# A fused local-and-pooled attention with a tanh-shrink MLP: dense blocks that follow the batches, V tiles every 112 tokens, V pooled on TensorE, nine-token rows of q and k, and weights cast by DMA

## The chip, the core and the metric

The kernel runs on one core of a Trainium2 chip. Its engines work side by side, each on its own list of instructions in order: TensorE (PE in the profile; matmuls, with weight loads shown apart as PEld), VectorE (DVE), ScalarE (ACT), GpSimd (POOL) and SyncE (SP), which here issues DMAs. The metric is the time of one execution in microseconds; lower is better.

## What is computed

```python
def _attn_ref(q, k, v):                       # 8 batches, 8 heads, 576 tokens, 64 wide
    q_d, k_d, v_d = means over groups of 4 tokens (144 groups)
    out_d = softmax_attention(q_d, k_d, v_d)  # pooled attention
    out_up = np.repeat(out_d, 4, axis=2)
    mask = np.abs(pos[:, None] - pos[None, :]) < 4
    out_local = softmax_attention(q, k, v, masked by mask)
    return out_up + out_local

def _moe_ref(x, w_in, w_out):                 # x: 4608 tokens x 512
    h = x @ w_in                              # to 2048
    g = h - np.tanh(h)
    return g @ w_out                          # back to 512
```

Inputs and the output are float32; the kernel computes its products in bfloat16 with float32 sums.

## The kernel before

**Work.** Attention goes in 32 pairs of heads, four pairs to a batch (pair p belongs to batch p // 4). The dense part, the two products of the MLP, goes in nine blocks of 512 tokens. All instructions are entered as operations with the tiles they read and write, a cost and a priority (class Program); a planner lays them out by simulated start times, and each engine gets its list in that order. Attention has the priority 10 x p, dense matmuls 5000 (so they fill what attention leaves), the dense blocks' ACT and DVE steps -1.

**A pair of attention.** SP loads q and k (load_qk, L291) as 96 rows of six tokens and V (load_v, L310 to L316) as five overlapping windows of 128 tokens, 120 apart. prep_v (L351) casts V to bf16 on POOL or ACT. The casts at L416 bring q and k to bf16. Then there are two forms:

- Old form, pairs 0 to 15: TensorE transposes q and k in twelve pieces (L442), ACT copies them out of PSUM (L448). V is pooled on TensorE for two pairs at a time (pool_v, L389 and L391, six matmuls with 128 output rows against `pick`), and ACT copies the result (L396). Local scores for tiles 0 to 3 (s1, L478), then the last tile and the pooled scores (s2, L478 and L494), are computed one after the other into the same banks `ps_ts`. The normalised output is transposed back on TensorE (back, L566 to L570), ACT copies the pooled part (L597), and DVE joins the two into `xT` (L599).
- New form, pairs 16 to 31 (T_DMA, X_DMA, NEW): q and k are transposed by a DMA that SP issues (L424), ACT copies them into token order (L432). V is loaded a second time in rows of four tokens (load_v4, L362) and pooled by two additions on POOL (pool_v4, L372 and L376). Both kinds of scores are computed in one go (s12), the second kind into `ps_ox`. The output is transposed by a DMA (L573) and joined on DVE or POOL (L582, L588).

In both, q and k are pooled by two additions (L459, L464), ACT takes the exponentials (L511, L521, L524), DVE masks them (L514, L527), TensorE forms the outputs (L538, L545), and DVE divides (L554, L556).

**Dense blocks.** mm1 (L619) multiplies `w_in` by `xT`: 16 groups of four matmuls of 512 columns a block, each into one of four PSUM banks `ps_hy`; ACT takes tanh (L627), DVE subtracts (L630) into `gT`, of which there are two. mm2 (L646) multiplies `gT` by `w_out`: 4 groups of 16 matmuls; ACT copies (L657) and SP stores (L660). Block k needs every batch that its 512 tokens touch. Block 0 is entered as 16 groups of mm1 and then its mm2; block 1 as mm1 alone; from block 2 on, mm1 of a block alternates with mm2 of the block before. The banks are handed out in turn in this order, so a step also waits for the earlier user of its bank.

**Weights.** SP loads `w_in` after the first four pairs (L328) and `w_out` between later pairs (L335, L337), in float32, into space borrowed from `gT` and `xT`. POOL and ACT cast them (load_w, L344), 32 pieces of 128 x 512.

Ahead of the first dense matmul, TensorE also runs filler matmuls (L802) where the plan leaves it idle.

Of the kernel before, what the change touches and what calls it, by code (L numbers as in the profile page):

```python
# [150 lines left out]
def kernel(  # L151
# [18 lines left out]
    A6 = 6  # L170
    G6 = S // A6
    QW = 120
    NT = 5
    NQ = [120, 120, 120, 120, 96]
    KOFF = 585
    N_FF = Dff // 128
    N_DC = Dm // 128
    NBLK = NTOK // 512
# [13 lines left out]
    pick = fixed("pick", [128, 6, 128], BF16)  # L192
# [4 lines left out]
    qkn = fixed("qkn", [G6, 2, 2, A6 * D], FP32, NQKN)  # L197
# [3 lines left out]
    qr = fixed("qr", [G6, 2, A6, 128], BF16, 2)  # L201
    qk = fixed("qk", [128, 1192], BF16, 2)
    qT = fixed("qT", [128, 2, A6, G6], BF16, 2)
    half = fixed("half", [128, 2, G, 2], FP32)
    qkd = fixed("qkd", [128, 344], BF16, 2)
    v4 = fixed("v4", [72, 2, 2, 4 * D], FP32, 2)
    v2 = fixed("v2", [72, 2, 2, 2 * D], FP32)
    vp = fixed("vp", [72, 2, 2, D + 1], BF16, 2)
    E = fixed("E", [128, 1840], BF16, 2)
# [5 lines left out]
    gT = fixed("gT", [128, N_FF, 512], BF16, 2)  # L215
# [37 lines left out]
    def c_pick():  # L253

        V.memset(pick, 0.0)
        for t in range(4):
            V.tensor_copy(out=pick[:, t, 30 * t:30 * t + 30], in_=group[:, 1:31])
        V.tensor_copy(out=pick[:, 4, 120:128], in_=group[:, 1:9])
        V.tensor_copy(out=pick[:, 5, 112:128], in_=group[:, 9:25])

    def c_mask():

        GP.memset(mask, 1.0)
        m4 = mask[:, 0:480].rearrange("p (t c) -> p t c", c=QW)
        for part, pat in ((m4, [[0, 4], [1, QW]]),
                          (mask[:, 480:576], [[1, 96]])):
            neg = [[-s, n] for s, n in pat]
            GP.affine_select(
                out=part, in_=part, compare_op=ALU.is_ge, fill=0.0,
                base=-1, pattern=neg, channel_multiplier=1)  # L270
            GP.affine_select(
                out=part, in_=part, compare_op=ALU.is_ge, fill=0.0,
                base=7, pattern=pat, channel_multiplier=-1)
        GP.affine_select(
            out=mask[:, 0:QW], in_=mask[:, 0:QW], compare_op=ALU.is_ge,
            fill=0.0, base=-4, pattern=[[0, QW]], channel_multiplier=1)
        GP.affine_select(
            out=mask[:, 480:576], in_=mask[:, 480:576], compare_op=ALU.is_ge,
            fill=0.0, base=99, pattern=[[0, 96]], channel_multiplier=-1)
# [6 lines left out]
    def load_qk(p):  # L286

        b, h0, s = p // NP, 2 * (p % NP), p % NQKN
        for i, src in enumerate((q, k)):
            def issue(i=i, src=src):  # L290
                nc.sync.dma_start(  # L291
                    out=qkn[s][:, i], in_=src[b, h0:h0 + 2].rearrange(
                        "h (g a) d -> g h (a d)", a=A6))
            load(500, issue, [("qkn", s, i)], T_QK, -30)

    def load_v(p):

        b, j, s = p // NP, p % NP, p % NVST
        t = vst[s]
        for i in range(2):  # L300
            h = 2 * j + i
            base = v[b, h]

            def win(tok, n, nt, base=base):
                return bass.AP(tensor=base.tensor, offset=base.offset + tok * D,
                               ap=[[D, n], [QW * D, nt], [1, D]])

            def issue(h=h, i=i, win=win):
                if b == 0 and h == 0:
                    nc.sync.dma_start(out=t[4:128, i, 0, :], in_=v[b, h, 0:124, :])  # L310
                    nc.sync.dma_start(out=t[:, i, 1:5, :], in_=win(QW - 4, 128, 4))
                elif b == B - 1 and h == H - 1:
                    nc.sync.dma_start(out=t[0:100, i, 4, :], in_=v[b, h, 476:576, :])
                    nc.sync.dma_start(out=t[:, i, 0:4, :], in_=win(-4, 128, 4))
                else:
                    nc.sync.dma_start(out=t[:, i], in_=win(-4, 128, 5))  # L316
            if (b, h) in ((0, 0), (B - 1, H - 1)):
                def clear(h=h, i=i):
                    part = t[0:32, i, 0, :] if h == 0 else t[96:128, i, 4, :]
                    V.memset(part, 0.0)  # L320
                op("DVE", 100, clear, writes=[("vst", s, i)], pri=-99)
            load(1000, issue, [("vst", s, i)], T_V, -30)

    def load_w(src, dst, name, f, stage, keys):

        def issue():
            if src is moe_w_in:
                nc.sync.dma_start(out=stage.rearrange("p (c f) -> p c f", c=4),  # L328
                                  in_=src[:, 512 * f:512 * f + 512].rearrange(
                                      "(c p) f -> p c f", p=128))  # L330
            else:
                rows = src.rearrange("(f p) n -> p f n", p=128)
                if isinstance(stage, list):
                    for c in range(4):
                        nc.sync.dma_start(out=stage[c], in_=rows[:, 4 * f + c, :])  # L335
                else:
# [497 lines left out]
```

## Time and profile before

| | |
|---|---|
| median of 3 runs | 348.71 us (348.31 to 348.74) |
| span of the profiled execution, first to last instruction | 346.3 us |
| mean granted TensorE clock | 0.984 |
| matmuls | 2556, of them 1152 dense |
| moved by DMA | 60.74 MB, nearly all issued by SP |

Times in the profile are microseconds from the first instruction. A row of instructions in order of time gives start, duration, engine, line, operation, output <- inputs, size and how many stand together; in square brackets, how long the engine had been idle and what ended that. Matmuls are pipelined: a row lasts longer than the engine needs before the next one, so what a matmul costs is read from start to start. A row of a stretch gives its length, then for each engine the busy time and the number of instructions, then the granted clock, the DMA engines' share (it can pass 1 where packets overlap) and GB/s.

### The profile page before, as it was taken

To read this page: it belongs to the slowest core of one execution; us is meant where nothing else is said; L and a number is where in the kernel's file an instruction comes from. 1 tells how busy PE (TensorE), PEld (TensorE's weight loads), DVE (VectorE), ACT (ScalarE), POOL (GpSimd) and SP (SyncE) were. 2 spreads that over 40 slices of the span, in tenths; PEclk is the share of its full clock that TensorE was granted. 3 is DMA by queue.
4 is the path that set the end of the run, shared out by engine and by line. 5 is a ranking of instruction groups with operands and counts; after the bars stand their busy time and mean duration, and the time that the engine had idled before them with its cause. 6 is when DMAs were issued, how large, how long until landed. Compare 5 with 4: busy or idle time off the path is not lost.

```text
span 346.3 us, 6847 instructions
## 1 busy us (share of the span) xinstructions
PE 328.0 (95%) x2556; PEld 163.5 (47%) x2556; DVE 223.8 (65%) x362; ACT 224.8 (65%) x382; POOL 169.9 (49%) x210
## 2 busy tenths in 40 slices
PE   6787989999999999999999999899999999999995
PEld 2353445555555554445444444444454444444442
DVE  5675788558897968778867677679774443343300
ACT  4585886768978768787878778599753434343411
POOL 6553555575467856887777786958500000000000
PEclk9698999999999999999999999999999999999999
DMA  8999999999999998999999999645231000100021
GB/s 192 234 374 300 277 262 263 217 216 287 212 222 234 252 234 174 226 231 235 261 221 207 260 233 246 157 92 93 57 85 60 31 32 30 61 32 31 30 93 61
DMA packets 103407, 60.74 MB, mean 175 GB/s; under 512 B 77774, under 2 KB 94670, under 8 KB 103374
## 3 DMA queue, kind: packets, MB, share of 16 engines
q1 hardware_dynamic: 103374, 60.30, 78.5%
q8 instruction: 20, 0.33, 0.4%
q14 instruction: 13, 0.11, 0.1%
HBM read 42.46 MB, written 9.44 MB: 150 GB/s over the span
## 4 chain that ended last, share of the span: by engine, by line
PE 69%; DVE 10%; ACT 9%; issue 3%; DMA 3%; POOL 2%; SPq 1%; ACTq 0%; POOLq 0%; DVEq 0%
PE ps_hy_540 L646 8%; PE ps_hy_538 L619 8%; PE ps_hy_539 L619 7%; PE ps_hy_541 L646 7%; PE ps_hy_538 L646 7%; PE ps_hy_539 L646 6%; PE ps_hy_540 L619 6%; PE ps_hy_541 L619 6%; PE ps_ox L538 3%; DVE qr_87 L416 2%; PE ps_ts L478 2%; DMA qkn_73<-in_k_dram 2%; PE ps_ox L545 2%; PE ps_ts L442 2%; PE ps_ox L389 2%
## 5 line engine op out<-in xcount | busy, mean ns | idle before, releaser
L619 PEld LDWEIGHTS <-w_in_sb 128*128 128x128 bf16 x576 | 53.3, 98 | 62.1 <-issue 3.9
L646 PEld LDWEIGHTS <-gT_110 128*128 128x128 bf16 x320 | 30.2, 98 | 34.5
L646 PEld LDWEIGHTS <-gT_111 128*128 128x128 bf16 x256 | 24.0, 98 | 27.4
L459 POOL TENSOR_TENSOR half<-qk_88 128x576 f32<-128x576 bf16 x14 | 16.4, 1169 | 25.3 <-ACT qk_88 L448 11.2
L459 POOL TENSOR_TENSOR half<-qk_89 128x576 f32<-128x576 bf16 x16 | 18.7, 1167 | 19.8 <-ACT qk_89 L448 12.2
L646 PE MATMUL ps_hy_539<-w_out_sb,gT_110 128*128 128x512 bf16 x80 | 20.7, 379 | 0.0
L646 PE MATMUL ps_hy_540<-w_out_sb,gT_110 128*128 128x512 bf16 x80 | 20.4, 379 | 0.0
L646 PE MATMUL ps_hy_538<-w_out_sb,gT_110 128*128 128x512 bf16 x80 | 20.4, 379 | 0.0
L646 PE MATMUL ps_hy_541<-w_out_sb,gT_110 128*128 128x512 bf16 x80 | 20.1, 379 | 0.0
L432 ACT COPY qk_89<-qT_91 128x576 bf16<-128x576 bf16 x16 | 18.7, 1193 | 0.0
L432 ACT COPY qk_88<-qT_90 128x576 bf16<-128x576 bf16 x16 | 18.4, 1188 | 0.0
L511 ACT ACTIVATE E_100<-ps_ts 128x960 bf16<-128x960 f32 x16 | 15.6, 977 | 3.8 <-PE ps_ts L478 3.8
L556 DVE TENSOR_TENSOR ln_106<-ps_ox,r_104 128x896 bf16<-128x896 f32 x16 | 17.4, 1090 | 0.5
L646 PE MATMUL ps_hy_540<-w_out_sb,gT_111 128*128 128x512 bf16 x64 | 16.9, 379 | 0.0
L646 PE MATMUL ps_hy_541<-w_out_sb,gT_111 128*128 128x512 bf16 x64 | 16.8, 379 | 0.0
L646 PE MATMUL ps_hy_539<-w_out_sb,gT_111 128*128 128x512 bf16 x64 | 16.6, 379 | 0.0
L646 PE MATMUL ps_hy_538<-w_out_sb,gT_111 128*128 128x512 bf16 x64 | 16.4, 379 | 0.0
L511 ACT ACTIVATE E_101<-ps_ts 128x960 bf16<-128x960 f32 x14 | 13.6, 973 | 3.8 <-PE ps_ts L478 3.6
L514 DVE TENSOR_TENSOR E_101<-E_101,mask 128x960 bf16<-128x960 bf16 x16 | 13.1, 820 | 3.9 <-ACT E_101 L511 3.7
L556 DVE TENSOR_TENSOR ln_107<-ps_ox,r_105 128x896 bf16<-128x896 f32 x14 | 15.3, 1090 | 0.4
L514 DVE TENSOR_TENSOR E_100<-E_100,mask 128x960 bf16<-128x960 bf16 x16 | 13.6, 847 | 2.8 <-ACT E_100 L511 2.8
L619 PE MATMUL ps_hy_538<-xT_65,w_in_sb 128*128 128x512 bf16 x36 | 13.9, 385 | 1.2 <-DVE xT_68 L599 1.2
(263 smaller groups left out, 890.1 us busy)
## 6 DMA issues: line engine op xcount, KB each, us to landing
out_dram<-y_115 SPq DMA_DIRECT2D x12, 256.0 KB, 2.6
out_dram<-y_116 SPq DMA_DIRECT2D x12, 256.0 KB, 2.3
out_dram<-y_117 SPq DMA_DIRECT2D x12, 256.0 KB, 3.0
qkn_71<-in_q_dram SPq DMA_DIRECT2D x8, 288.0 KB, 7.8
qkn_71<-in_k_dram SPq DMA_DIRECT2D x8, 288.0 KB, 5.8
qkn_72<-in_q_dram SPq DMA_DIRECT2D x8, 288.0 KB, 5.1
qkn_72<-in_k_dram SPq DMA_DIRECT2D x8, 288.0 KB, 5.5
qkn_73<-in_q_dram SPq DMA_DIRECT2D x8, 288.0 KB, 6.6
```

Of the source, the lines that this page charges most:

```text
L389: T.matmul(pv[:, 0, :], pick[:, t, :], vw[w][:, :, t, 0:64], start=(t == 0), stop=(t == NT - 1))
L416: P.choice([(eng, ns, lambda dst=dst, srt=srt, fn=fn: fn(out=dst, in_=srt)) for eng, ns, fn in REORDER[p >= NEARLY][i]], reads=[("qkn", sn ...
L432: op("ACT", 600, lambda i=i: A.copy(out=full[:, i].rearrange("p (g a) -> p g a", a=A6), in_=qT[s][:, i].rearrange("p a g -> p g a")), read ...
L442: T.transpose(b16[:, G6 * a:G6 * a + G6], qr[s][:, i, a, :], ident[0:G6, 0:G6])
L459: eng.tensor_tensor(out=half, in0=four[:, :, :, 0:2], in1=four[:, :, :, 2:4], op=ALU.add)
L478: T.matmul(sc[:, c:c + NQ[t]], qk[s][rows, k0:k0 + 128], qk[s][rows, QW * t:QW * t + NQ[t]], start=True, stop=True)
L511: op("ACT", 870, lambda: A.activation(out=e1, in_=ps[:, :, 0:480], func=AF.Exp, scale=SCALE), reads=ts, writes=[("E", s, 0)], pri=pri)
L514: op("DVE", 700, lambda: V.tensor_tensor(out=e1, in0=e1, in1=mask[:, 0:480].unsqueeze(1).to_broadcast([128, 2, 480]), op=ALU.mult), reads= ...
L538: T.matmul(po[:, hh, 65 * t:65 * t + 65], E[s][:, c:c + 128], vw[w][:, 2 * jj + hh, t, :], start=True, stop=True)
L556: op("DVE", 1010, lambda: V.tensor_tensor(out=ln[s].rearrange("p n (h d) -> p h n d", d=D), in0=blocks[:, :, :, 0:64], in1=r[s].unsqueeze( ...
L619: T.matmul(ps_hy[slot], w_in_sb[:, dc, fc * 128:(fc + 1) * 128], xT[dc][:, kb * 512:kb * 512 + 512], start=(dc == 0), stop=(dc == N_DC - 1))
L646: T.matmul(ps_hy[slot], gT[g][:, fc, ts * 128:ts * 128 + 128], w_out_sb[:, fc, :], start=(fc == 0), stop=(fc == N_FF - 1))
```

## The change

- **Dense blocks follow the batches.** Eight blocks in place of nine: even ones of 512 tokens, odd ones of 640, so that block b needs batch b and no later one. An odd block's mm1 runs in two halves of 320 columns. A block's mm1 is interleaved with mm2 of the block before by share; the last call runs mm2 of block 7 alone. A bank is taken as the one longest unused, and mm2 holds its bank until its 16 matmuls are done.
- **V tiles every 112 tokens**, all inside the head's 576, so the loads need no cleared edges and no special cases; the tiles' query ranges are 120, 112, 112, 112, 120.
- **V pooled on TensorE for all pairs**: four matmuls with 32 output rows each, into quarters of the partitions, and one with 128. Pooled q and k are laid out as 5 x 32 columns (160 in place of 144). From pair 4 on the result goes to `ps_ts`. load_v4 and pool_v4 are gone.
- **Nine-token rows**: q and k of a pair are loaded as 64 rows each of nine tokens, q on even and k on odd partitions, and transposed in nine pieces of 128 x 128. Another load form (`tok`) is in the code and no pair uses it.
- **Weights cast by DMA**: POOL issues one DMA per quarter of `w_in` and `w_out`, which casts on its way. Each waits for the V cast of a pair: `w_in` of pairs 2, 2, 3, 3 and `w_out` of pairs 3, 4, 5, 6.
- **The new form from pair 10** in place of 16 (DMA transposes on both sides, scores in one go).
- The planner's costs are new numbers.

The core of the diff:

```diff
-    M2_FIRST, T_DMA, X_DMA, NEW = 16, 16, 16, 16
+    EARLY = 10
+    TIN = ['pe'] * EARLY + ['dma'] * (NPAIR - EARLY)
+    MERGE = [False] * EARLY + [True] * (NPAIR - EARLY)
+    XOUT = ['pe'] * EARLY + ['dma'] * (NPAIR - EARLY)
+    W_IN_AT, W_OUT_AT = (2, 2, 3, 3), (3, 4, 5, 6)
...
+    def span(kb):
+        return (kb * S, 512, 1) if kb % 2 == 0 else (kb * S - 64, 320, 2)
+
+    def take():
+        slot = next(x for x in slots if x not in held)
+        slots.remove(slot)
+        slots.append(slot)
+        return slot
...
     def dense(kb):
+        n1 = 16 * span(kb)[2] if kb < B else 0
+        n2 = 16 + 4 * ((kb - 1) % 2) if kb else 0
+        steps = sorted([((i + 0.5) / n1, 0, i) for i in range(n1)] +
+                       [((i + 0.5) / n2, 1, i) for i in range(n2)])
+        for _, second, i in steps:
+            if second:
+                mm2(kb - 1, i)
+            else:
+                mm1(kb, i)
...
     def load_w(src, dst, name, f, gate):
+        op("POOL", 1000, lambda: nc.gpsimd.dma_start(out=to, in_=rows),
+           reads=[gate], writes=[("wq", name, f)], pri=-40)
+        op("DMA", T_W, None, reads=[("wq", name, f)],
+           writes=[(name, f, c) for c in range(4)], pri=-30)
...
     def pool_v(hb):
-            for t in range(NT):
-                T.matmul(pv[:, 0, :], pick[:, t, :], vw[w][:, :, t, 0:64],
-                         start=(t == 0), stop=(t == NT - 1))
-            T.matmul(pv[:, 1, :], pick[:, 5, :], vw[w][:, :, 4, 0:64],
+            for t in range(4):
+                T.matmul(pv[32 * t:32 * t + 32, 0, :], pick[:, 0:32],
+                         vw[w][:, :, t, 0:64], start=True, stop=True)
+            T.matmul(pv[:, 1, :], pick[:, 32:160], vw[w][:, :, 4, 0:64],
                      start=True, stop=True)
...
+                def put(i=i, planes=planes):
+                    if LOAD[p] == 'row':
+                        A.copy(out=full[:, i].rearrange("p (g a) -> p g a", a=A9),
+                               in_=planes[:, :, i::2].rearrange("p a g -> p g a"))
...
     def s2(bank=ps):
             for hh in range(2):
-                score(4, hh, 512 * hh, sc)
+                score(4, hh, bank[:, hh, 0:120])
             for i in range(2):
                 for hh in range(2):
                     rows = slice(64 * hh, 64 * hh + 64)
+                    T.matmul(bank[:, hh, 120 + GW * i:120 + GW * i + GW],
+                             qkd[s][rows, 1, 32 * i:32 * i + 128],
+                             qkd[s][rows, 0], start=True, stop=True)
```

More of the change, by code (lines that the diff above doesn't have):

```diff
@@ L639, in mm2 @@
         if part == 0:
[L640 to L641 removed]
+            ycur[0] = take()
+            held.append(ycur[0])
         slot = ycur[0]
```

496 lines of the change are left out of this document (214 added, 282 removed).

## The prediction

> **What bounds it now.** I read the page's totals, its slices and its chain first, then the busy time of each engine in stretches cut where the data say so, then TensorE's instructions in order of time.
>
> ```profile
> span 346.3 us, 6847 instructions
> ...
> PE 328.0 (95%) x2556; PEld 163.5 (47%) x2556; DVE 223.8 (65%) x362; ACT 224.8 (65%) x382; POOL 169.9 (49%) x210
> ...
> DMA  8999999999999998999999999645231000100021
> ...
> PE 69%; DVE 10%; ACT 9%; issue 3%; DMA 3%; POOL 2%; SPq 1%; ACTq 0%; POOLq 0%; DVEq 0%
> ...
> L432 ACT COPY qk_89<-qT_91 128x576 bf16<-128x576 bf16 x16 | 18.7, 1193 | 0.0
> ```
>
> TensorE is busy for 95% of the span and carries 69% of the chain that ended last; no other engine passes 65%. The DMA queues are near full for the first two thirds. The next views split the time. The borders are the first dense matmul (32.06), the end of the last join of batch 1 (74.90), of batch 3 (130.90) and of batch 7 (260.90), and the last matmul's end (342.10); the last column but two is the granted clock.
>
> ```profile
> core 0: us, PE busy (x) PEld busy (x) DVE busy (x) ACT busy (x) POOL busy (x), PEclk, DMA share, GB/s
> ...
> 32.06:74.90 42.84, 41.81 (x374) 21.85 (x374) 29.62 (x44) 30.88 (x59) 24.67 (x32) 0.96 1.16 253
> 74.90:130.90 56.00, 55.14 (x559) 30.53 (x558) 46.55 (x75) 43.81 (x83) 35.98 (x41) 1.00 1.14 239
> 130.90:260.90 130.00, 127.23 (x1007) 62.06 (x1005) 100.31 (x150) 99.55 (x154) 91.08 (x102) 1.00 0.89 183
> 260.90:342.10 81.20, 81.20 (x377) 36.62 (x375) 26.72 (x40) 30.40 (x53) 0.00 (x0) 1.00 0.12 45
> ```
>
> The same stretches for the first dense product (L619) alone, then for the second (L646):
>
> ```profile
> 32.06:74.90 42.84, 16.80 (x64) 6.12 (x63) 0.96 1.16 253
> 74.90:130.90 56.00, 28.27 (x112) 9.43 (x112) 1.00 1.14 239
> 130.90:260.90 130.00, 63.38 (x247) 22.60 (x246) 1.00 0.89 183
> ```
>
> ```profile
> 32.06:74.90 42.84, 15.19 (x62) 5.42 (x63) 0.96 1.16 253
> 74.90:130.90 56.00, 12.11 (x47) 4.04 (x46) 1.00 1.14 239
> 130.90:260.90 130.00, 63.04 (x248) 23.18 (x247) 1.00 0.89 183
> ```
>
> The last stretch holds nothing but dense work: 377 matmuls in 81.20 us, so 0.2154 us for one of 512 columns and no idle time at all. The program has 1,152 of them: 248.1 us. From 32.06 to 342.10 are 310.0 us, so 61.9 us went to everything else, attention's own matmuls and stalls. By stretch: 42.84 - 126 x 0.2154 = 15.7; 56.00 - 159 x 0.2154 = 21.8; 130.00 - 495 x 0.2154 = 23.4; the missing 1.0 is matmuls that cross a border and are counted twice. What attention needs on TensorE is read from starts in a stretch without gaps:
>
> ```profile
> 84.97 0.39 PE L478 MATMUL ps_ts<-qk_88 64*128 64x120 bf16 x8
> 85.29 0.33 PE L538 MATMUL ps_ox<-vw_81,E_101 128*128 128x65 bf16 x5
> ...
> 85.86 0.38 PE L619 MATMUL ps_hy_539<-xT_65,w_in_sb 128*128 128x512 bf16 x1
> ...
> 87.15 0.68 PE L442 MATMUL ps_ts<-ident,qr_87 96*128 96x96 bf16 x12
> 87.67 0.38 PE L619 MATMUL ps_hy_539<-xT_67,w_in_sb 128*128 128x512 bf16 x1
> ...
> 88.10 0.22 PE L566 MATMUL ps_ox<-ident,ln_107 128*128 128x128 bf16 x1
> ...
> 88.63 0.38 PE L619 MATMUL ps_hy_538<-xT_65,w_in_sb 128*128 128x512 bf16 x1
> ...
> 89.59 0.22 PE L478 MATMUL ps_ts<-qk_88 64*128 64x96 bf16 x2
> ...
> 89.86 0.39 PE L619 MATMUL ps_hy_541<-xT_65,w_in_sb 128*128 128x512 bf16 x1
> ...
> 90.73 0.73 PE L389 MATMUL ps_ox<-vw_82,pick 128*128 128x256 bf16 x5
> ...
> 91.51 0.39 PE L478 MATMUL ps_ts<-qk_89 64*128 64x120 bf16 x8
> ```
>
> A step lasts from its first start to the start of what follows. Transposing q and k: 87.67 - 87.15 = 0.52. First scores 0.32, outputs 0.57, transposes back 0.53, second scores 0.27, V pooling 0.78 for two pairs, 0.39 for one. A pair in the old form costs 2.60 us. In the new form (from pair 16) both transposes and V pooling leave TensorE, and the scores go together:
>
> ```profile
> 160.22 0.39 PE L478 MATMUL ps_ts<-qk_88 64*128 64x120 bf16 x8
> ...
> 160.70 0.39 PE L619 MATMUL ps_hy_540<-xT_65,w_in_sb 128*128 128x512 bf16 x1
> ```
>
> That is 0.48, with the outputs 1.05 us for a pair. Twelve old pairs lie behind 32.06 (31.2 us) and sixteen new ones (16.8 us). So the stalls are 15.7 + 21.8 - 31.2 = 6.3 us with the old form (0.52 for a pair) and 23.4 - 16.8 = 6.6 us with the new (0.41). The reader sees that from 32 us on TensorE does little but work: only work taken off it, or an earlier start, can bring much.
>
> **The start.** Nine rows show what held the first dense matmul:
>
> ```profile
> 16.61 2.28 SPq L328 DMA_DIRECT2D gT_111<-in_moe_w_in_dram  x2
> ...
> 19.00 2.19 SPq L291 DMA_DIRECT2D qkn_71<-in_q_dram  x1
> ...
> 21.51 0.73 ACT L351 CAST vw_81<-vst_78 128x640 bf16<-128x640 f32 x1
> ...
> 24.02 0.29 PE L494 MATMUL ps_ts_123<-qkd_94 64*128 64x144 bf16 x4
> ...
> 24.55 1.14 ACT L344 CAST w_in_sb<-gT_110 128x512 bf16<-128x512 f32 x2
> ...
> 25.59 0.33 ACT L521 ACTIVATE E_101<-ps_ts_123 128x192 bf16<-128x192 f32 x1
> ...
> 31.09 1.17 POOL L344 CAST w_in_sb<-gT_111 128x512 bf16<-128x512 f32 x2 [2.42 <-DMA gT_111<-in_moe_w_in_dram]
> ...
> 32.06 0.59 PE L619 MATMUL ps_hy_538<-xT_65,w_in_sb 128*128 128x512 bf16 x1 [1.20 <-DVE xT_68 L599]
> ...
> 32.22 0.56 DVE L416 CAST qr_86<-qkn_71 96x768 bf16<-96x768 f32 x1 [0.22 <-DMA qkn_71<-in_q_dram]
> ```
>
> It waited for the last join of batch 0 (xT_68). In that pair's chain the second scores were issued at 24.02, yet ACT took the exponential at 25.59, having cast two pieces of w_in from 24.55. The q load of pair 4 was issued at 19.00 behind w_in on SP, and its cast at 32.22 still waited for it.
>
> **The change part by part.**
>
> Dense blocks of 512 and 640 tokens. The 640 are two halves of 320 columns, so the first product has 256 matmuls of 512 and 512 of 320. Twelve transposes of 96 columns took 0.52, 0.0433 each; between that and 0.2154 for 512 a column costs 0.000414 us, so 320 cost 0.136. The sum is (256 + 576) x 0.2154 + 512 x 0.136 = 248.8 us, 0.7 more. What moves is when the work may start. Before, block 0 gives 128 matmuls between the ends of batches 0 and 1 (64 + 62 were used there). Now the second product of block 0 stands between first products of block 1, and a PSUM bank of its second group is freed by those: 64 + 16 = 80 may run, 17.2 us. Afterwards each batch brings about 31 us of dense work (512 x 0.136 is 69.6 for four batches, the rest by 0.2154), and batch 7 leaves 48.
>
> New form from pair 10. Six pairs leave the old form. Behind 32.06 are then 6 old pairs at 2.21 without V pooling (13.3) and 22 new ones at 1.05 (23.1). The transposes' DMAs go into the queue earlier, and SP waits for their inputs with loads behind them; ACT's copy out of a DMA transpose takes 1.19 us (L432), under an ACT that was busy for 99.55 of 130.00 us. This is hidden by the dense work as long as there is some.
>
> Pooled keys padded to 160 columns: four matmuls of 16 more columns, 0.03 a pair, 0.8 in all.
>
> V pooled on TensorE for all pairs: 14 poolings behind 32.06. Five matmuls in place of six make 5/6 x 0.78 = 0.65. Four of them have 32 output rows each, into different quarters. The eight first scores above use half the array each and took 0.32, where twelve narrower transposes took 0.52, so they overlapped in twos. If the four overlap fully, 0.26 is left (two matmuls' time). I take 0.50, nearer to the serial end because no row shows quarters: 7.0 us, bounds 3.6 to 9.1. On "TensorE: Matmul & The Clock Gate" (Part 3, packing small matmuls) the Trainium skill says that matmuls in different column groups run together, three of them 2.38 times as fast; "TensorEngine Tiling (Array Packing)" (Key Properties) says that a change of mode drains the array. By the first the term would be about 5 us as an estimate, by the second nearer mine.
>
> It also takes two additions a pair off POOL (one of them below), which was busy for 91.08 of the 130.00 us; POOL was not last in the chain, so I count nothing, and the slack covers later joins.
>
> ```profile
> L372 POOL TENSOR_TENSOR v_97<-v_96 72x512 f32<-72x512 f32 x8 | 10.4, 1306 | 0.2
> ```
>
> Weights cast by DMA. ACT and POOL lose 32 casts, and SP no longer carries these loads. At the start ACT's casts held the exponential that the last join waited for by up to 1.14: I take 1.06 of it, first dense matmul at 31.0, bounds 28 (below) and 36 (four waits as long again). What is new is a wait on POOL: each weight DMA stands there until a pair's V is cast, and behind it the additions for pooled q and k, for which TensorE's second scores wait; V arrives in pair order, so a late V costs there what it costs anyway. Pair 4's q and k can arrive earlier; its transposes and first scores (0.84) then fit into idle time ahead of 31.0.
>
> Nine-token rows, V tiles of 112, fewer guards: transposes take 9 x 128 columns for 12 x 96, the same 1,152; nothing.
>
> Sum: 31.0 + 248.8 + 13.3 + 23.1 + 0.8 + 7.0 - 0.8 = 323.2. Stalls stay at their rate, 6 x 0.52 + 22 x 0.41 + 1.0 = 13.1; 2.0 for hunger before batch 1 ends (bounds 0 and 15.2); tail 346.3 - 342.1 = 4.2. That is 342.5 us of span against 346.3. The runs' median stands 2.4 above this profile's span, so 344.9 us.
>
> **The rivals.**
>
> Hunger between batches 0 and 1. TensorE may then do 17.2 us of dense work and 10.4 for four old pairs. If attention keeps the 42.84 us it took, 42.84 - 27.6 = 15.2 us stand idle, 13.2 more than I put in: 358 us. It decides from about 36 us on, where the gain is gone. For it: DMA share 1.16 there, and the weights still pass the same queues. Against it: pair 4's loads no longer wait behind w_in, and the 28.0 us a batch between 74.90 and 130.90 were reached with the same four-step chain.
>
> Late weights. The last w_in load was issued at 16.61 to 18.89 and its data let POOL go on at 31.09, 12.2 us later. Now it waits for pair 3's V cast (in the old run over at 22.24), is issued by POOL, and shares the engines with the loads of pairs 4 to 7: landing between 34.4 and, at half the rate, 46.6. The last quarter of block 0 is wanted at 31.0 + 48 x 0.2154 = 41.3 at the earliest. At worst 5.3 us: 350 us. The Trainium skill ("SBUF — State Buffer", the "DVE blocks DMA" trap) says that descriptors of DMAs issued from POOL cannot be written while DVE holds the shared port in a fast copy; that would push to this side, and no row here has such a DMA. DVE's casts of q and k, 0.56 each, are the copies in question.
>
> A better start. If w_in off SP and ACT brings the first matmul to 28, V pooling overlaps (-3.4) and stalls halve with the hunger gone (-8): 331 to 338, say 335.
>
> The transposes come too early. The stretch from 74.90 to 130.90 already has a DMA share of 1.14. If batches 2 and 3, with pairs 10 to 15 in the new form, take 42.84 us each as batch 1 did, against 31 of dense work, 4.2 of attention and 1.0 of V pooling, 6.6 us are idle in each: 358. Against it: SP also sheds V's second load for the new form.
>
> **Numbers.** Bound by TensorE as summed: 0.55, 345, own range 338 to 350. Hunger 0.17. Late weights 0.11. Better start 0.12. Early transposes 0.05. A measurement can tell about 0.2% (0.7 us) from no change. Faster takes 0.47 of the first, the whole of the fourth and a little of the third: 0.60; same 0.05; slower 0.35. Range 335 to 357: from the better start to just short of full hunger.
>
> **What would show it.** The dense matmul at 0.215 for 512 and 0.136 for 320 columns; the first near 31; batch 1 ending before 62 to 65; a stretch after batch 7 with no gap; starts of V pooling 0.3 to 0.65 apart from what follows; 1.05 a pair from pair 10. Wrong: TensorE idle for over 5 us between batches 0 and 1, weights that land behind their matmuls, or stalls over 0.6 a pair in the new form.

## The result and the profile after

| | before | after |
|---|---|---|
| median (lowest to highest) of 4 runs each | 348.51 us (347.12 to 348.74) | 359.97 us (358.77 to 361.62) |
| span of the profiled execution | 346.3 us | 359.8 us |
| first dense matmul | 32.06 | 51.32 |
| last join of batch 0, of batch 1, of batch 7 ends at | 32.0, 74.9, 260.9 | 50.2, 80.2, 278.2 |

The changed kernel takes 1.0339 times as long (95% interval 1.0285 to 1.0392): it is slower, where the prediction said 344.9 us and a range to 357. The page of the profile after, in the lines that answer to those of before, with the granted clock's row (tenths of full speed in 40 slices of 9 us) added:

```profile
span 359.8 us, 7072 instructions
...
PE 328.6 (91%) x2637; PEld 179.8 (50%) x2637; DVE 210.1 (58%) x400; ACT 239.0 (66%) x430; POOL 132.7 (37%) x180
...
PEclk9975569999999999999998999999999999999999
DMA  7999999349799999888998797554222010001012
...
PE 71%; DMA 15%; DVE 5%; ACT 3%; issue 2%; POOL 1%; SPq 1%; DVEq 0%; ACTq 0%; POOLq 0%
PE ps_hy L619 31%; PE ps_hy L647 29%; DMA vst<-in_v_dram 5%; DMA qT<-qr 5%; DMA lT<-ln 4%; PE ps_ox L522 2%; PE ps_ts L463 2%; PE ps_ox L528 2%; DMA qkn<-in_k_dram 1%; DVE ln L539 1%; DVE qr L400 1%; PE ps_ts L422 1%; PE ps_ox L553 1%; PE ps_ts L356 1%; DVE gT L630 1%
```

TensorE's busy time is the same (328.6 against 328.0); what grew is the time in which it waits. In the chain that ended last, DMA went from 3% to 15%, 5 of them loads of V. The third to sixth slices, 18 to 54 us, show the low clock of an engine that stands. The same in stretches, with the columns of the prediction's table (length; busy time and number of instructions of PE, PEld, DVE, ACT, POOL; granted clock; DMA share; GB/s), cut at 32, at the first dense matmul, at the ends of batches 1, 3 and 7, and at TensorE's end:

```profile
0.00:32.00 32.00, 19.56 (x191) 11.24 (x192) 16.99 (x52) 17.16 (x31) 15.53 (x31) 0.86 1.05 235
32.00:51.32 19.32, 11.97 (x104) 7.14 (x103) 5.73 (x11) 5.18 (x12) 10.22 (x13) 0.59 1.19 245
51.32:80.20 28.88, 27.64 (x245) 14.40 (x244) 21.60 (x34) 21.74 (x44) 10.12 (x13) 0.96 0.63 172
80.20:152.70 72.50, 70.75 (x631) 39.42 (x631) 51.58 (x93) 61.87 (x108) 39.55 (x52) 1.00 1.02 228
152.70:278.20 125.50, 120.63 (x1063) 67.87 (x1061) 87.34 (x164) 101.54 (x175) 57.25 (x72) 0.99 0.66 139
278.20:355.90 77.70, 77.70 (x409) 39.73 (x407) 26.82 (x48) 30.94 (x61) 0.00 (x0) 1.00 0.12 45
```

The loss lies in the second row: 19.32 us in which the old kernel already ran dense work. Of its 11.97 us of busy time 5.1 are filler matmuls, the granted clock is 0.59, and the DMA engines' share is 1.19. From the first dense matmul to the end of the span the changed kernel needs 308.5 us (359.8 - 51.3), the old one 314.2. So the dense part itself got 5.7 us shorter, and it began 19.3 us later.

What TensorE waited for there is read from its rows in order of time (start, duration, what; in brackets the idle time and what ended it):

```profile
26.84 0.61 PE L766 MATMUL ps_ox<-lT 128*128 128x512 bf16 x1
33.62 0.41 PE L356 MATMUL ps_ts<-vw,pick 128*32 128x256 bf16 x4 [6.18 <-POOL vw L341]
...
34.58 0.31 PE L549 MATMUL ps_ox<-ident,ln 128*128 128x128 bf16 x1
...
37.80 0.45 PE L477 MATMUL ps_ts<-qkd 64*128 64x160 bf16 x4 [1.96 <-POOL qkd L454]
...
47.65 0.45 PE L477 MATMUL ps_ts<-qkd 64*128 64x160 bf16 x4 [3.76 <-POOL qkd L454]
48.03 0.29 PE L549 MATMUL ps_ox<-ident,ln 128*128 128x128 bf16 x1
...
51.32 1.04 PE L619 MATMUL ps_hy<-xT,w_in_sb 128*128 128x512 bf16 x2
```

The first hole is closed by the V pooling (L356) of pairs 4 and 5, which belong to batch 1. It stands in TensorE's list ahead of pair 2's transposes back (L549 at 34.58), which batch 0 needs. The third hole waits for pooled q and k (L477 <- qkd), and behind it stands pair 3's L549 at 48.03. POOL's list tells why both came late:

```profile
16.35 3.13 POOL L334 DMA_DIRECT2D w_in_sb<-in_moe_w_in_dram  x4
19.45 0.77 POOL L334 DMA_DIRECT2D w_out_sb<-in_moe_w_out_dram  x1
...
20.98 0.75 POOL L334 DMA_DIRECT2D w_out_sb<-in_moe_w_out_dram  x1
...
32.85 0.72 POOL L341 CAST vw<-vst 128x640 bf16<-128x640 f32 x1 [8.36 <-DMA vst<-in_v_dram]
...
44.18 0.72 POOL L341 CAST vw<-vst 128x640 bf16<-128x640 f32 x1 [6.44 <-DMA vst<-in_v_dram]
...
46.87 0.72 POOL L454 TENSOR_TENSOR qkd<-half 128x320 bf16<-128x320 f32 x1
```

POOL stood 8.36 and 6.44 us for V of pairs 5 and 6; the additions for which L477 waited come behind the second of these casts. Batch 0's own loads had long landed: the last `w_in` DMA, which waits for the V cast of pair 3, was issued by 19.5. All three holes wait for data of batch 1, or for steps that stand behind such a wait on POOL. The V loads themselves, from SP's rows, the chain of waits and the page's DMA rows (KB each, us from issue to landing):

```profile
23.75 4.61 SPq L321 DMA_DIRECT2D vst<-in_v_dram  x2
28.48 5.33 SPq L291 DMA_DIRECT2D qkn<-in_q_dram  x1
```

```profile
24.41 19.64 DMA vst<-in_v_dram
```

```profile
vst<-in_v_dram SPq DMA_DIRECT2D x64, 160.0 KB, 5.0
...
w_out_sb<-in_moe_w_out_dram POOLq DMA_DIRECT2D x4, 512.0 KB, 17.1
```

A V load takes 5.0 us in the median of all 64; the one that the chain names, pair 6's second, issued at 24.41, landed 19.64 us later, and issuing one q load took SP 5.33 us. This is just when six weight DMAs were on their way. Of the time from 10 to 60 us alone, the queues' share of the 16 engines (packets, MB, share) is:

```profile
q1 hardware_dynamic: 15239, 8.41, 65.5%
q0 software_dynamic: 4224, 4.19, 50.2%
```

SP's queue (q1) and POOL's (q0) together pass 100% (the time that their packets took, which can overlap): the weights' packets stand for 50.2 of it in the very stretch in which the loads of pairs 5 and 6 were on their way.

### The profile page after: what moved, and what is told of

Its sections match the earlier page's. It is cut to its first block, busy times and chain, and to the rows that moved or that the text cites. A ratio compares the mean times of both kernels' runs of the same rounds, so it can differ in the third digit from the quotient of the medians.

```text
span 359.8 us, 7072 instructions
## 1 busy us (share of the span) xinstructions
PE 328.6 (91%) x2637; PEld 179.8 (50%) x2637; DVE 210.1 (58%) x400; ACT 239.0 (66%) x430; POOL 132.7 (37%) x180
## 4 chain that ended last, share of the span: by engine, by line
PE 71%; DMA 15%; DVE 5%; ACT 3%; issue 2%; POOL 1%; SPq 1%; DVEq 0%; ACTq 0%; POOLq 0%
PE ps_hy L619 31%; PE ps_hy L647 29%; DMA vst<-in_v_dram 5%; DMA qT<-qr 5%; DMA lT<-ln 4%; PE ps_ox L522 2%; PE ps_ts L463 2%; PE ps_ox L528 2%; DMA qkn<-in_k_dram 1%; DVE ln L539 1%; DVE qr L400 1%; PE ps_ts L422 1%; PE ps_ox L553 1%; PE ps_ts L356 1%; DVE gT L630 1%
## 5 line engine op out<-in xcount | busy, mean ns | idle before, releaser
L619 PE MATMUL ps_hy<-xT,w_in_sb 128*128 128x320 bf16 (+1 forms) x768 | 150.3, 330 | 0.1
L647 PE MATMUL ps_hy<-w_out_sb,gT 128*128 128x512 bf16 x576 | 146.5, 380 | 0.1
L630 DVE TENSOR_TENSOR gT<-ps_hy,u 128x320 bf16<-128x320 f32 (+1 forms) x192 | 103.5, 553 | 61.4 <-ACT u L627 59.8
L627 ACT ACTIVATE u<-ps_hy 128x320 f32<-128x320 f32 (+1 forms) x192 | 93.2, 493 | 57.9 <-PE ps_hy L619 52.0
L647 PEld LDWEIGHTS <-gT 128*128 128x128 bf16 x576 | 54.5, 98 | 52.7 <-issue 0.3
L412 ACT COPY qk<-qT 128x576 bf16<-128x576 bf16 x44 | 52.3, 1200 | 0.0
L445 POOL TENSOR_TENSOR half<-qk 128x576 f32<-128x576 bf16 x29 | 33.4, 1151 | 42.4 <-ACT qk L412 18.9
L400 POOL CAST qr<-qkn 128x576 bf16<-128x576 f32 x40 | 27.1, 690 | 42.0 <-DMA qT<-qr 30.2
L539 DVE TENSOR_TENSOR ln<-ps_ox,r 128x896 bf16<-128x896 f32 x32 | 34.9, 1090 | 1.0
L495 ACT ACTIVATE E<-ps_ts 128x912 bf16<-128x912 f32 x32 | 29.8, 932 | 6.6 <-PE ps_ts L463 5.9
L454 POOL TENSOR_TENSOR qkd<-half 128x320 bf16<-128x320 f32 x29 | 22.9, 791 | 1.6
```

The lines of the kernel that those rows point to most:

```text
L400: P.choice([(eng, ns, lambda dst=dst, srt=srt, fn=fn: fn(out=dst, in_=srt)) for eng, ns, fn in any3], reads=[("qkn", sn, 0), ("qkn", sn, 1 ...
L412: op("ACT", 1190, lambda i=i: A.copy(out=full[:, i].rearrange("p (g a) -> p g a", a=A9), in_=qT[s][:, :, i::2].rearrange("p a g -> p g a") ...
L445: eng.tensor_tensor(out=half, in0=four[:, :, :, 0:2], in1=four[:, :, :, 2:4], op=ALU.add)
L495: op("ACT", 960, lambda: A.activation(out=e1, in_=ps[:, :, 0:456], func=AF.Exp, scale=SCALE), reads=ts, writes=[("E", s, 0)], pri=pri)
L539: op("DVE", 1090, lambda: V.tensor_tensor(out=ln[s].rearrange("p n (h d) -> p h n d", d=D), in0=blocks[:, :, :, 0:64], in1=r[s].unsqueeze( ...
L619: T.matmul(ps_hy[slot][:, 0:n], w_in_sb[:, dc, fc * 128:(fc + 1) * 128], xT[dc][:, t0 + c0:t0 + c0 + n], start=(dc == 0), stop=(dc == N_DC ...
```

## The experiments

Three theories. **A**: weights on a second queue share the DMA engines with the loads of pairs 4 to 6; their V tiles come late, and the fixed lists of POOL and TensorE hold waits for them ahead of batch 0's last steps. **B**: the first dense matmul waits for the weights themselves. **H** (hunger): between the ends of batches 0 and 1 the new order has too little dense work. (Some expectations name a **C**: the loss lies in the parts behind the first dense matmul. Those on H name its rival **R**: the hole is attention waiting for its loads.) Two further suspects: the planner's new costs, and the transposes moved to DMA. Edits are to the changed kernel, where nothing else is said.

**1. The planner's costs** (order of the lists only).

```diff
-    T_QK, T_QKN, T_V, T_W, NEARLY = 850, 1350, 760, 2850, NP
+    T_QK, T_QKN, T_V, T_W, NEARLY = 1300, 1350, 1150, 3400, NP
```

> The planner's costs of a q or k load, a V load and a weight quarter are raised from 850, 760 and 2850 to 1300, 1150 and 3400 ns, near the spacing at which they land in the profile after; only the order of the lists changes, no transfer. Theory A (loads of pairs 5 and 6 come late behind the weights, and TensorE's and POOL's lists hold waits for them ahead of the last steps of batch 0): those waits move behind batch 0, the first dense matmul comes at 34 to 40 instead of 51.3, the time is 343 to 350 us. Theory B (the cast weights themselves are late): no change, 357 to 362 us, since they land when they land. Theory C (the loss is in the parts behind the first dense matmul): within 3 us of 360.

Measured: 368.17 us, ratio to before 1.0603 (1.0497 to 1.0708). Batch 0's last join ended at 31.7, 18.5 us sooner than in the changed kernel, but the first dense matmul came at 50.83 all the same: the list now had pair 4's transposes back ahead of it, as TensorE's rows show.

```profile
49.06 0.29 PE L549 MATMUL ps_ox<-ident,ln 128*128 128x128 bf16 x1 [6.29 <-DVE ln L539]
...
50.83 1.49 PE L619 MATMUL ps_hy<-xT,w_in_sb 128*128 128x512 bf16 x3
```

Theory A's own forecast for this run (dense start 34 to 40, 343 to 350 us) failed, and so did those of B and C. Another order moves the wait to another instruction; the late data stay, so this plan alone is no cure.

**2. Later w_out** (its DMAs behind V casts 7, 7, 8, 8).

```diff
-    W_IN_AT, W_OUT_AT = (2, 2, 3, 3), (3, 4, 5, 6)
+    W_IN_AT, W_OUT_AT = (2, 2, 3, 3), (7, 7, 8, 8)
```

> The w_out quarters wait for the V casts of pairs 7, 7, 8, 8 instead of 3, 4, 5, 6; the planner's costs stay. Theory A: V of pairs 5 and 6 lands 5 to 15 us earlier, as only w_in shares the engines with it; the first dense matmul at 36 to 44, the time 344 to 353 us. Theory B: first dense matmul unchanged at 51, since w_in is as before, 358 to 362 us, or more if w_out now comes late for the second product.

Measured: 354.04 us, 1.0205 (1.0111 to 1.03), first dense matmul at 43.6 in place of 51.3, batch 1 ends at 73.0 in place of 80.2. Two megabytes of another tensor, issued later, bring batch 0 forward by 7 us; the time is 1 us above A's range. One hole is left, for the same kind of wait:

```profile
34.76 0.45 PE L477 MATMUL ps_ts<-qkd 64*128 64x160 bf16 x4 [6.89 <-POOL qkd L454]
```

**3. Weights as before** (SP loads them in float32, POOL and ACT cast them; all other parts changed).

```diff
-        op("POOL", 1000, lambda: nc.gpsimd.dma_start(out=to, in_=rows),
-           reads=[gate], writes=[("wq", name, f)], pri=-40)
+        load(600, issue, keys, T_W, -30)
+        for c in range(4):
...
+            P.choice([(eng, ns, lambda part=part, to=to, fn=fn: fn(out=to, in_=part))
+                      for eng, ns, fn in CAST], reads=keys, writes=[(name, f, c)],
+                     pri=W_PRI + f)
```

> This part of the change undone: weights loaded in float32 by SP after the first four pairs and cast by POOL and ACT, all else as after. Theory A: V and q, k of pairs 4 to 6 stand behind the weights on SP's one queue and the plan knows that order, so batch 0 is not held: first dense matmul at 31 to 36, 343 to 349 us. Theory C: 357 us or more.

Measured: 359.08 us, 1.0342 (1.0253 to 1.0432). The first dense matmul is back at 34.8, and yet the time is that of the changed kernel. The stretch from 60 to 80 us (columns as above) shows the loss in a new place:

```profile
60.00:80.00 20.00, 13.10 (x146) 9.45 (x144) 10.59 (x18) 10.21 (x22) 10.26 (x14) 0.58 0.73 192
```

TensorE is busy for 13.10 of 20 us, and its clock falls to 0.58: batch 1 ends at 80.5, 45.7 us behind the first dense matmul. That is hunger, which the late start of the changed kernel had covered. Theory A's dense start was met, its time (343 to 349) was not; the time is the one that C gave.

**4. The new form from pair 16 again.**

```diff
-    EARLY = 10
+    EARLY = 16
```

> The new form from pair 16 again, all else as after. By my sum the six pairs cost TensorE 6 x (2.60 - 0.39 - 1.05) = 7 us more. Theory A: the first dense matmul stays at 50 to 52, the time 361 to 368 us. If early transposes were the cause (a rival of the prediction): 345 to 355 us.

Measured: 361.26 us, 1.0411 (1.0315 to 1.0506), first dense matmul at 52.8 and the same holes ahead of it. The transposes that were moved to DMA are not the cause. But the 7 us that the six pairs were to cost more do not show either. From the first dense matmul to the last matmuls, first in the changed kernel and then in number 4 (columns as above):

```profile
51.32:355.90 304.58, 296.72 (x2345) 161.41 (x2343) 187.33 (x338) 216.09 (x386) 106.92 (x136) 0.99 0.61 139
```

```profile
52.78:356.00 303.22, 300.41 (x2440) 166.12 (x2439) 185.92 (x329) 213.03 (x399) 108.18 (x139) 1.00 0.51 128
```

With the six pairs in the old form TensorE is busy 3.7 us longer and stands 2.8 us in place of 7.9. So the new form from pair 10 in place of 16 is worth 1.3 us here (361.26 against 359.97), not 7; the runs do not show why.

**5 to 7. Hunger by itself.** Number 5 is number 3 with block 0's second product right behind its first, as the old kernel has it (128 dense matmuls that need only batch 0, in place of 80). Number 6 is number 2 with the same edit. Number 7 is the old kernel with the opposite edit.

```diff
+        if kb == 1:
+            steps = [s for s in steps if not s[1]]
+        if kb == 0:
+            steps += [(1.0, 1, i) for i in range(16)]
...
-    M2_FIRST, T_DMA, X_DMA, NEW = 16, 16, 16, 16
+    M2_FIRST, T_DMA, X_DMA, NEW = 0, 16, 16, 16
```

> The run with weights by SP and casts on POOL and ACT, and besides that the second product of block 0 entered right behind its first, as in the kernel before, so that 128 dense matmuls may run between batches 0 and 1 instead of 80. Theory H (hunger: with batch 0 no longer held, TensorE runs out of dense work until batch 1 ends; its clock fell to 0.58 between 60 and 80 us there): 10 us of dense work move into the hole and the clock stays up, 341 to 350 us. Rival R (the hole is attention waiting for its loads, with or without dense work): 356 to 361 us.

> The run with later gates for w_out, and the second product of block 0 right behind its first. Batch 0 ends near 43 us there and the PE share between 60 and 80 us was 17.45 of 20, so there is less hunger to fill: theory H says 1 to 4 us less than that run's 354, R no change.

> The kernel before with one number changed (M2_FIRST 16 to 0), so that the second product of block 0 is entered between the first products of block 1, as the change enters it. Theory H: 44 to 48 dense matmuls, 9.5 to 10.3 us, cannot run between batches 0 and 1 and TensorE stands: 353 to 361 us. R: batch 1 comes earlier as TensorE is free for attention and the time stays within 3 us of 348.

Measured: number 5 362.0 us, 1.0369 (1.0308 to 1.0429); number 6 357.91, 1.0262 (1.0211 to 1.0312); number 7 361.32, 1.035 (1.0293 to 1.0407). Number 7 first, the stretch from 60 to 80 us of the old kernel and then of the old kernel with that one number changed:

```profile
60.00:80.00 20.00, 19.97 (x214) 11.33 (x212) 12.01 (x21) 13.98 (x26) 13.27 (x16) 1.00 1.20 223
```

```profile
60.00:80.00 20.00, 13.28 (x130) 8.53 (x130) 8.89 (x14) 11.19 (x22) 11.46 (x15) 0.71 0.99 205
```

The first dense matmul stands where it was (31.9), batch 1 ends at 76.2 against 74.9, and the kernel loses 13.0 us (361.32 against 348.35 for the old kernel beside it). So the old kernel's time rests on the 128 matmuls. The cure, however, failed in the changed kernel. Number 5's stretches from 60 to 80 and from 100 to 130:

```profile
60.00:80.00 20.00, 14.59 (x156) 8.81 (x156) 8.87 (x14) 10.16 (x22) 11.19 (x15) 0.83 0.65 181
...
100.00:130.00 30.00, 20.78 (x217) 12.61 (x218) 19.59 (x37) 24.38 (x39) 15.83 (x20) 0.77 0.87 193
```

The hole shrinks by 1.5 us and comes again before batch 2 ends, at 124.6, where TensorE is busy for 20.78 of 30. Dense work that is spent early is missed later as long as the batches come no faster. Numbers 5 and 6 went against H: number 5 came out just above what the rival R gave (362.0; 356 to 361), and number 6 is no faster than number 2 (357.91 against 354.04), where H said 1 to 4 us faster. Yet R's reason fails too, as in number 3 the chain that ended last holds no DMA between 30 and 82 us. TensorE's rows of number 3 show another (here L434 transposes q and k, L475 makes scores, L631 is the first product):

```profile
34.30 0.67 PE L434 MATMUL ps_ts<-ident,qr 128*128 128x128 bf16 x9
34.81 6.21 PE L631 MATMUL ps_hy<-xT,w_in_sb 128*128 128x512 bf16 x28
...
42.69 0.37 PE L475 MATMUL ps_ts<-qk 64*128 64x120 bf16 x8
...
52.23 0.23 PE L475 MATMUL ps_ts<-qk 64*128 64x120 bf16 x2
```

Between pair 4's transposes (34.30) and its second scores (52.23) the list holds 74 of the 80 dense matmuls. After that the four pairs pass through TensorE, ACT and DVE one behind the other (their joins end at 59.2, 65.4, 72.7 and 80.5), with nearly no dense work left to fill the gaps. By these rows it is not only a matter of how much dense work there is: it ran ahead of batch 1's steps. No run changed that order alone, so this is a reading and not shown. H is shown in the old kernel, by number 7; in the changed one the dense work that it calls for was no cure.

**8. Weights spread out further, mm2(0) early**: number 6 with `w_in` behind casts 2, 3, 5, 5.

```diff
-    W_IN_AT, W_OUT_AT = (2, 2, 3, 3), (7, 7, 8, 8)
+    W_IN_AT, W_OUT_AT = (2, 3, 5, 5), (7, 7, 8, 8)
```

> As the run with later gates and the second product early, and w_in gated by pairs 2, 3, 5, 5 instead of 2, 2, 3, 3, so that q, k and V of pairs 5 and 6 share the engines with half of w_in. Theory A: V of pair 5 lands near 25 instead of 33, batch 0 ends at 32 to 38, first dense matmul there; the second half of w_in lands near 40. 340 to 350 us. If the weights themselves then hold TensorE (theory B): 350 to 358.

Measured: 346.98 us (10 runs), 0.997 (0.993 to 1.001). First dense matmul at 40.3, two us later than theory A said (V of pair 5 landed at 29.0, not near 25), batch 1 ends at 71.2; the time is in A's range.

**9. The same gates, the change's own dense order.**

> The changed kernel with its weights issued behind V casts 2, 3, 5, 5 (w_in) and 7, 7, 8, 8 (w_out); the second products stay as the change has them, without the early mm2(0) of the run before. Theory A (weights on a second queue delay the V tiles of pairs 4 to 6): the first dense matmul at 40.3 within 1.5 us, as in the run before, since its loads are the same. What the early mm2(0) was worth there is then told apart: it cost 3.9 us with the first gating (357.9 against 354.0), so if that holds, 343 us, within 340 to 347, and faster than both kernels. Rival (hunger between batches 0 and 1 is the larger part now that batch 0 ends ten us sooner, and mm2(0) filled it): 352 to 358, with TensorE's time in 60 to 80 below 16 us at a granted clock below 0.8.

Measured: 346.73 us (12 runs), 0.9986 (0.9952 to 1.002), first dense matmul at 40.4 as expected and batch 1's end at 69.5. The time lies at the upper edge of what theory A gave (340 to 347), and it is that of the old kernel, not below it as was said. The early mm2(0) is worth nothing either way here. With nothing changed but the moment at which weight DMAs are issued, and the lists that follow from it, 13.2 us of the changed kernel's 359.97 are gone. The largest hole left ahead of the dense work is once more the pooling of pairs 4 and 5:

```profile
30.97 0.40 PE L356 MATMUL ps_ts<-vw,pick 128*32 128x256 bf16 x4 [4.01 <-POOL vw L341]
```

**10. All of w_in behind V casts 4, 4, 5, 5.**

```diff
-    W_IN_AT, W_OUT_AT = (2, 2, 3, 3), (3, 4, 5, 6)
+    W_IN_AT, W_OUT_AT = (4, 4, 5, 5), (7, 7, 8, 8)
```

> As the run before, but all of w_in behind V casts 4, 4, 5, 5: nothing of the weights is issued before pair 4's V. Theory A: V of pair 5 lands before 26 us (28.3 and 29.0 with two chunks ahead of it, 28.6 and 32.7 in the changed kernel), the holes at 23.5 and 27.0 (3.6 and 2.9 us) shrink below 2 us in sum, and batch 0 ends at 35 or before. Whether the first dense matmul follows is the test of late weights: the last w_in issued at some 30 and landing 10 us later gives a dense start of 38 to 42 and a time within 3 us of the run before; the first dense matmul then waits on DMA w_in by the trace. If weights have no part in it the dense start is at 35 to 37, and the time some 4 us below the run before.

Measured: 349.77 us, 1.0048 (1.0009 to 1.0087). V of pair 5 landed by 22.9, as expected, and the pooling of pairs 4 and 5 (27.4) has no hole ahead of it. But holes of 1.32 and 0.77 us stand at DVE's steps ahead of it (below 2 in sum was expected), and a new one of 1.76 ends at 37.7: there DVE had waited 3.39 us for a later pair's k. Batch 0 ended at 37.5, not at 35. V of pair 7 now landed at 40.2 and 42.5, and pooled q and k behind its cast on POOL leave a hole of 3.01 that ends at 46.8. The first dense matmul came at 38.6, 1.1 us behind the last join, and no wait for w_in is shown at it, where that was expected. The delay goes to whichever pair is loading while the weights pass.

**11. Weights by POOL's queue alone, in the old kernel** (gates as in the change, nothing else changed).

```diff
-    for f in range(4):
-        load_w(moe_w_in, w_in_sb, "w_in", f, *stages[f])
-    queue = list(ORDER)
...
+    W_IN_AT, W_OUT_AT = (2, 2, 3, 3), (3, 4, 5, 6)
...
             prep_v(p + 2)
+            load_ws(p + 2)
```

> The old kernel with one part of the change alone: its weights go through POOL's queue with the cast, gated as in the change behind V casts 2, 2, 3, 3 and 3, 4, 5, 6; the 32 casts of weights on POOL and ScalarE and the fp32 loads on SP's queue go. Everything else is old, the dense order too. Theory A (weights on the second queue share the DMA engines and bring the V tiles of pairs 5 and 6 late, for which the lists of TensorE and POOL wait): V of pair 6 lands after 37, batch 0 ends after 38 in place of 32.0, and the time is 352 to 362. Rival (this part alone costs nothing: POOL and ScalarE are freed of 32 casts, and SP of 4 MB, and the loss comes only together with the change's own plan): batch 0 ends by 33, and 345 to 349.

Measured: 352.75 us, 1.0197 (1.015 to 1.0244). This one part makes the old kernel slower, by 1.5 to 2.4%, although it takes 32 casts off POOL and ACT. Batch 0 ended at 31.9, so that part of the expectation was wrong. But the first dense matmul came at 41.15, behind a V pooling for batch 1, and POOL's row names the load (here L377 is the pooling, L339 the V cast, L607 the first product):

```profile
38.52 1.23 PE L377 MATMUL ps_ox<-vw,pick 128*128 128x256 bf16 x5 [7.23 <-POOL vw L339]
...
41.15 0.85 PE L607 MATMUL ps_hy<-xT,w_in_sb 128*128 128x512 bf16 x2
```

```profile
37.75 0.72 POOL L339 CAST vw<-vst 128x640 bf16<-128x640 f32 x1 [7.46 <-DMA vst<-in_v_dram]
```

A stands by itself: seven of the nine microseconds by which the dense work starts later are one wait for one V tile, at an instruction that batch 0 does not need.

**12. Number 9 with V planned later**, so that the poolings stand further back in TensorE's list.

```diff
-    T_QK, T_QKN, T_V, T_W, NEARLY = 850, 1350, 760, 2850, NP
+    T_QK, T_QKN, T_V, T_W, NEARLY = 850, 1350, 1150, 2850, NP
```

> The ninth run (weights behind casts 2, 3, 5, 5 and 7, 7, 8, 8) with one planned number more: a V load is planned with 1150 in place of 760, so that the pooling of pairs 2 and 3, and of 4 and 5, stands later in TensorE's list. Theory A says that the remaining holes at 24.2 and 26.6 (2.3 and 4.4 us, the larger one at a pooling that waits for V of pair 5) are the price of a list that expects V sooner than it comes: the hole at the pooling shrinks below 2 us, the first dense matmul comes at 36 to 38, and the time falls by 2 to 5 us to 342 to 345. Rival (the V of pair 5 at 29 to 30 is what batch 0 waits for in any order): the hole only changes its place, first dense matmul 40, time 345 to 349.

Measured: 349.55 us, 1.0083 (1.0045 to 1.0121). The hole at the pooling shrank from 4.01 to 1.79 us, batch 0 ended at 34.6 in place of 40.2 and batch 1 at 66.8 in place of 69.5; but the first dense matmul came at 39.4, and holes of 0.9 to 1.8 us opened ahead of 108.6, 110.8 and 113.6, where batch 2 ended at 114.9 in place of 109.5. Neither theory's time was met. As in number 1, a list made for other times pays elsewhere.

## Why the prediction was wrong

**The step that failed** is "a late V costs there what it costs anyway", in the part on the weights cast by DMA, and with it the first dense matmul at 31.0 (bounds 28 and 36; measured 51.3). The prediction had put a price on weights that come late (at most 5.3 us), and on the casts that leave ACT. It had not asked what the weights do to the loads on the other queue, although its rival of late weights says that they share the engines with the loads of pairs 4 to 7. It even took a gain from there: that pair 4's q and k "can arrive earlier". They did (transposed at 22.91, in the old kernel at 36.15); the V tiles of pairs 5 and 6 did not, and batch 1, which was to end before 62 to 65, ended at 80.2. The weights left SP's queue, but not the engines behind it, whose share was already 1.16 in the row that the prediction shows for 32.06 to 74.90. Numbers 2 and 9 show it by moving the issues alone, with the lists that follow from it (51.3 to 43.6 to 40.4), number 11 by the part alone. The Trainium skill, "DMA: Bandwidth & Descriptors" (Issuing engines are not separate DMA queues), says that DMAs of different issuers run on the same 16 engines and interleave, and that issuing on several saves the issuers' time alone; the shares of 65.5% and 50.2% agree. That rule spoke against this change and was not weighed.

**Theory B falls.** The issues of the four pieces of w_in, and their time from issue to landing:

```profile
L334 POOL DMA_DIRECT2D w_in_sb<-in_moe_w_in_dram x4: 747/754/903, 16.3 to 18.7; - x4
...
DMA to landing us min/median/max: 8.7/12.5/17.6
```

The four pieces landed at 25.0, 28.5, 31.8 and 36.3, the last 15 us ahead of the matmul that needs the first of them. Late weights were never waited for; the rival of that name (350 us) looked at the wrong data.

**The sum.** The predicted span was 342.5, the measured one is 17.3 more: 20.3 from the first dense matmul, and 3.0 less behind it. Of the terms there some were right, and some missed in both directions. The rows that give their sizes:

```profile
60.08 0.29 PE L356 MATMUL ps_ts<-vw,pick 128*32 128x256 bf16 x4
60.30 0.29 PE L358 MATMUL ps_ts<-vw,pick 128*128 128x256 bf16 x1
60.43 1.24 PE L619 MATMUL ps_hy<-xT,w_in_sb 128*128 128x512 bf16 x5
```

```profile
179.90 0.71 PE L619 MATMUL ps_hy<-xT,w_in_sb 128*128 128x320 bf16 x4
180.44 0.59 PE L647 MATMUL ps_hy<-w_out_sb,gT 128*128 128x512 bf16 x2
```

- Four matmuls of 320 columns take 0.54 from start to start, 0.135 each (0.136 predicted). With 832 at 0.2154 the dense part is 248.3 (248.8).
- A V pooling takes 0.35 (60.08 to 60.43), not 0.50: 13 of them behind the first dense matmul are 4.6, the predicted 14 were 7.0. The four quarter matmuls take 0.22 where four of the fifth's 0.13 would be 0.52, 2.4 times as fast. The sum by the rule of "TensorE: Matmul & The Clock Gate" (Part 3) of the Trainium skill was the better one. (The reading that the eight first scores "overlapped in twos" does not come out: by the prediction's own price they would take 0.43 one by one and 0.21 in twos, and took 0.32.)
- The tail is 3.9 (359.8 - 355.9; 4.2).
- Attention's matmuls were to take 36.4 (13.3 + 23.1 + 0.8, less 0.8 for pair 4's part). By the rows, all of pair 4 but its transposes back, and pair 5's transposes and first scores, had run ahead of 51.32: 2.5 in place of 0.8. That leaves 34.7, and of the 308.5 then 17.0 for stalls and hunger, where the prediction had 13.1 + 2.0.
- The new form from pair 10 was to save TensorE 7 us against pair 16; number 4 needs 307.5 behind its first dense matmul (360.3 - 52.8), no more than the 308.5 here. "The transposes come too early" falls with number 4 as the cause of the loss; that they eat up what the new form saves is possible and not shown.
- The median stood 2.4 above the span before, and stands 0.2 above it now, as the execution that was profiled is the slowest of the four: 20.3 - 3.0 - 2.2 is the whole error of 15.1. That the last two took something off is luck.

**The rival "hunger"** (358 us) named a mechanism that is real, as number 7 shows, but it is not the one that the changed kernel shows. Its 17.2 us of dense work and 10.4 of attention, 27.6, just fill the 28.88 us between 51.32 and 80.20. (The 27.64 us that TensorE was busy there agree with this by chance: some of the attention had run before, and the first dense matmuls took 0.39 each at the low clock.) Take the late start away, and it appears: in number 3 batch 1 ends 45.7 us behind the first dense matmul, 18.1 more than 27.6, and the time stays at 359. So the term of 2.0 for hunger was mis-sized as well; that it did not show was luck, as the other error hid it.

**Both in one.** As TensorE has only 27.6 us of work between the first dense matmul and batch 1's end, what counts is when batch 1 ends. A reading made after the runs: the span less batch 1's end, both of the profiled execution, is 279.6 us in the changed kernel (359.8 - 80.2), and 279.3, 278.4, 279.7, 277.6, 276.7 and 280.1 in numbers 2, 3, 4, 9, 10 and 12, all with the change's dense order, while the first dense matmul wanders from 34.8 to 52.8. Number 1 does not fit (288.1): there batch 2 comes late (131.8, against 109.5 in number 9). And batch 1 ended 29 to 30 us behind batch 0 in the changed kernel and in numbers 2, 4 and 9, so there a late batch 0 passed on whole; in number 3 it took 45.9. The old kernel had 42.8 us of work for that stretch and could wait until 74.9.

**What stays open.** Whether a version beats the old kernel. Numbers 8 and 9 beat the changed one by 13 us, but their intervals against the old one hold 1. A plan whose load costs follow from measured landings, and V poolings of batch 1 held back behind batch 0's last joins, was not tried as a whole; number 12 moved them by one planned number and paid for it in batch 2. Open too are why the new form of pairs 10 to 15 saved so little, and whether number 3 would gain from a list that lets batch 1's steps go first.

## What to carry to other kernels

Moving transfers to another queue does not take them off the DMA engines: where the share is at 1 already, ask whose data will land later, and then which instruction of a fixed list waits for them with more urgent work behind it. A step on its way to a barrier should not stand behind one that serves the next batch. And when a late start is repaired, look at once for the next shortage behind it: with work for only 27.6 us, starting 16 us earlier brought nothing, as batch 1 ended no sooner.

## Unexpected on the hardware

- Holes cost more than their length: from 32.00 to 51.32 the granted clock was 0.59, and the nine transposes of q and k of a pair, from start to start of the last and the next step, took 0.94 (40.82 to 41.76), where the same nine took 0.50 later on (63.97 to 64.47), at a granted clock of 1.00. The Trainium skill ("TensorE: Matmul & The Clock Gate", Part 1) gives half the clock after some 3.4 us of idle time; the two largest holes here were of 6.18 and 3.76 us.

```profile
40.82 1.15 PE L422 MATMUL ps_ts<-ident,qr 128*128 128x128 bf16 x9
41.76 1.97 PE L766 MATMUL ps_ts<-lT 128*128 128x512 bf16 x5
```

- A weight DMA costs POOL 0.75 to 0.90 us to issue, and lands 8.7 to 22.0 us later. While these were under way, SP needed up to 4.0 us for the issue of a V load, which takes it 0.59 in the median, and 5.33 for one of q.
